# Scores of three sequences moved to the transposes' PSUM banks, with the first stage's steps in another order

## The chip, the cores and the metric

One core of a Trainium2 chip runs the whole kernel. The metric is device time in microseconds (us), the median of three runs; lower is better. One further execution was taken with the hardware profiler. PE is TensorE (matmuls), DVE VectorE, ACT ScalarE, POOL GpSimd, and SP the engine whose queue issues the DMAs here.

## The reference, cut to what matters

An mLSTM cell over 4 batches ("sequences" below) of 8 heads, 768 steps and 40 columns, followed by a two-layer product with an exact GELU between:

```
for t in range(S):                       # per batch and head
    m_new = max(f[t] + m, i[t]);  f_ = exp(f[t] + m - m_new);  i_ = exp(i[t] - m_new)
    C = f_ * C + i_ * outer(v[t], k[t]);  n = f_ * n + i_ * k[t]
    y[t] = sigmoid(o[t]) * (C @ q[t]) / max(abs(n @ q[t]), 1)
x = y.transpose(0, 2, 1, 3).reshape(3072, 320)
out = gelu(x @ w_in) @ w_out             # w_in 320 x 2048, w_out 2048 x 320
```

## The kernel before, in words

The 768 steps are cut into 6 chunks of 128. Within a chunk the recurrence becomes matrix products per sequence: keys and queries are transposed on PE, scores are products of keys and queries (L542), weighted by exponentials W of the gates; the weighted scores meet the values; the state C of the earlier chunks is read and updated; then the output is gated and transposed into x. While one chunk goes through the cell, the chunk before it goes through the two layers: "up" (x by w_in, then Gelu) and "down" (by w_out).

The order of instructions is written out by hand. `play` (L1184) reads a string of words; a word is a letter for a step and a number for the sequence (or the piece) it works on. Each engine executes its own instructions in the order in which the steps issue them, and a wait holds everything behind it on its engine. DMAs stand in SP's queue in the same way. The string FRONT (L27) covers the first chunk's cell, the second chunk's cell, the first chunk's up and down, and the preparation of both weight matrices. DOWN (L34) orders the later chunks, one after another. The change touches FRONT alone and one line of `scores`.

Letters that matter here; lower case is the first chunk, upper case the second:

- m/M masks a W tile on POOL (L440). It comes from DRAM, by `load_M` (L177), in the second chunk and after; word B issues such a load ahead of time. w/W are the exponentials on ACT (L443).
- t/T: four transposes of k and four of q on PE into two banks of the pool `ps_tr`, each copied out on ACT (L514 to L525). `ps_tr` has two banks in all. In the second chunk, T also issues the product of v by a gate on DVE (L529).
- s/S: scores, eight products on PE into two banks, then a product with W on DVE (L532 to L545).
- c/C: products for state and read on PE (L580, L585), then on ACT, or in the second chunk on DVE (L589 to L600).
- v/V: weighted scores by values on PE (L660) into a bank of `ps_h`, and in the second chunk a sum on DVE (L668). y/Y: the gated output, five operations and a copy on DVE (L678 to L696). x/X: its transposes on PE (L707) and a copy on ACT; in the second chunk the bank is in `ps_tr`, and R (L725) on DVE is the last that reads it. g/G: the tanh of the output gate on ACT (L474).
- P fetches a piece of a weight matrix. K and J, each time for the next piece, turn its 64-bit numbers into float32: K on ACT (L373, L374), J on DVE (L385, L386); J also fetches a later piece. Pieces 0 to 9 are w_in, 10 to 25 are w_out. i splits a piece of w_in into a high and a low part (ACT L768, DVE L769), j joins them (DVE L788), h and Z prepare the next up.
- A and U: up-products of the first chunk's first and second half of tokens (L872, L878) into banks "a" or "b" of `ps_mm`, then Gelu on ACT (L882). f2, f3: the rest of that up-product, 24 and 12 products into all four banks of `ps_mm` (L811, L817), then Gelu on ACT (L823). u splits x for them.
- F: one of the 16 rows of the first chunk's down-product (L1111); from F0 on it holds all four banks of `ps_mm`.
- L and O load q, k and v, o_gate. e writes the third chunk's k and q to DRAM and reads them back as blocks. I n puts n idle matmuls into the next bank that a step opens (`unread`, L397); k n puts n matmuls on PE (`warm`, L222).
- E, N, D, Q, d, q compute and transpose the gates; E and N store M to DRAM.

The eight PSUM banks are two of `ps_tr`, two of `ps_h`, and two each of tags "a" and "b" of `ps_mm`. Before the change, the scores of the second chunk's sequences 0 and 2 use "a", those of 1 and 3 `ps_tr` (L540).

Of the kernel before, what the change touches and what calls it, by code (L numbers as in the profile page):

```python
# [24 lines left out]


FRONT = """  # L27
    O0 P0 I4 L0 E P1 I4 P2 w0 L1 t0 O1 L2 k5 K L3 N g0 k2 s0 J w1 D O3 w2 t1 K c0 v0 y0 Q O2 I1 I1 s1 d w3 q
    P3 t2 v1 g1 c1 L4 K J y1 x0 s2 g2 x1 O4 t3 J v2 c2 y2 s3 B4 g3 K x2 B5 T0 v3 J H K y3 K A L5 c3 x3 M1 O7
    O6 K M0 O5 J J u0 u1 G0 L6 W0 S0 i5 W1 A K C0 T1 J J M2 i6 V0 G2 u2 U i7 L7 S1 K G1 K U j5 J j6 j7 i8 W2  # L30
    C1 J K B8 T2 i9 f2 M3 V1 T3 j8 K S2 J h5 Y0 Y1 j9 W3 J C2 K h6 S3 C3 f3 J K Z r X0 J K J K J K V2 V3 h7 K
    F K F Y2 J F K J K J e J G3 R0 h8 J F Z F F X1 F K K F X2 F R1 F J K F J J Y3 K X3 R2 F F F J B9 p R3 F K
    J h9 B10 F"""
DOWN = """  # L34
    M0 F Z F L3 W0 M1 Z W1 S0 C0 F F h0 Q2 F K2 G1 D3 B3 Z V0 G2 M2 W2 M3 W3 V1 K3 Q3 F G0 S2 Z Y0 G3 C2 h2 F
    F Y1 X0 V2 V3 F N F j R0 Y2 Y3 X1 F F X2 R1 F R2 X3 R3 F"""
# [3 lines left out]
def kernel(  # L40
# [18 lines left out]
    B, H, S, D = q.shape  # L59
# [26 lines left out]
    ps_tr = ctx.enter_context(tc.tile_pool(name="ps_tr", bufs=2, space=bass.MemoryType.PSUM))  # L86
    ps_h = ctx.enter_context(tc.tile_pool(name="ps_h", bufs=2, space=bass.MemoryType.PSUM))
    ps_mm = ctx.enter_context(tc.tile_pool(name="ps_mm", bufs=2, space=bass.MemoryType.PSUM))
# [121 lines left out]
    a = gates.tile([BH, NCH, L], F32, name="a")  # L210
# [82 lines left out]
    def decays_last(g0, g1):  # L293
        g = slice(g0, g1)
        pd = ps_tr.tile([P, g1 - g0, BH], F32, name="pd", tag="tr")
        nc.tensor.matmul(pd.rearrange("p c n -> p (c n)"), last, gT[:, g].rearrange("p c n -> p (c n)"),
                         start=True, stop=True)
        by_half = pd.rearrange("p c (n two) -> p c n two", two=2)
        for hip in range(2):
            nc.vector.tensor_copy(out=dec[halves[hip], g], in_=by_half[halves[hip], :, :, hip])  # L300
# [65 lines left out]
    def conv_one(i):  # L366

        if i < len(pieces):
            n = bits[i].shape[1]
            lo, hi = bits[i][:, :, 0], bits[i][:, :, 1]  # L370
            s = sig[i] = raw.tile([P, WP], F32, name="sig", tag="sig")[:, 0:n]
            p = pow2[i] = raw.tile([P, WP], U32, name="pow", tag="pow")[:, 0:n]
            nc.scalar.activation(out=s, in_=hi.bitcast(F32), func=AF.Copy, scale=2.0 ** -112)  # L373
            nc.scalar.activation(out=p, in_=lo, func=AF.Relu, scale=0.9 * 2.0 ** -29, bias=low_bits)  # L374
# [4 lines left out]
    def conv_two(i):  # L379

        if i < len(pieces):
            bits.pop(i)
            to = sig[i] if 4 < i < 10 else pieces[i][1]
            dst, s, p = to.bitcast(U32), (sig[i] if 4 < i < 10 else sig.pop(i)).bitcast(U32), pow2.pop(i)
            nc.vector.scalar_tensor_tensor(out=p, in0=s, scalar=3, in1=p, op0=OP.logical_shift_left, op1=OP.bitwise_or)  # L385
            nc.vector.scalar_tensor_tensor(out=dst, in0=s, scalar=0x80000000, in1=p, op0=OP.bitwise_and, op1=OP.bitwise_or)  # L386
            if i != HELD:
                fetch(i + NB - (i > HELD))
# [8 lines left out]
    def unread(bank):  # L397
        for _ in range(idle[0]):
            nc.tensor.matmul(bank, ident, ident, start=True, stop=True, skip_group_check=True)
        idle[0] = 0  # L400
# [25 lines left out]
    class Cell:  # L426
# [105 lines left out]
        def scores(self, b):  # L532
            n = self.c * B + b
            kT, qT = self.kT.pop(b), self.qT[b]

            pool, tag = (ps_tr, "tr") if self.c > 0 and b % 2 else (ps_mm, "a")
            ps = [pool.tile([P, NP, L], F32, name="ps", tag=tag) for hip in range(2)]
            unread(ps[0][:, 0, :])
            for p in range(NP):
                for hip in range(2):  # L540
                    r = halves[hip]
                    nc.tensor.matmul(ps[hip][:, p, :], kT[r, p, :], qT[r, p, :], start=True, stop=True)  # L542
            for hip in range(2):
                w = W[n].rearrange("p (m two) t -> p m two t", two=2)[:, :, hip, :]
                nc.vector.tensor_tensor(out=w, in0=ps[hip], in1=w, op=OP.mult)  # L545
# [340 lines left out]
    def first_up_steps(h):  # L886

        def step(k):
            ups.append((len(ups) + len(tags_next) % 2, (2 * k, 2 * k + 2, HT * h, HT * h + HT)))
            if len(ups) == 2:  # L890
                first_up()

        return [lambda k=k: step(k) for k in range(HF // 2)]
# [209 lines left out]
    def first_down_steps(g):  # L1103
        po = []

        def row(f):

            if f == 0:
                po.extend(ps_mm.tile([P, DM], F32, name="po", tag="ab"[b // 2]) for b in range(B))
            for b in range(B):  # L1110
                nc.tensor.matmul(po[b], g.t[:, f, b * L:(b + 1) * L], w_out[:, f, :], start=(f == 0),  # L1111
                                 stop=(f == NF - 1))
                if f == NF - 1:
                    if b % 2 == 0:
                        o_sb = outp.tile([P, 2, DM], F32, name="o_sb", tag="o_sb")
                    nc.scalar.copy(out=o_sb[:, b % 2, :], in_=po[b])
                    send(0, b, o_sb[:, b % 2, :])

        return [lambda f=f: row(f) for f in range(NF)]
# [71 lines left out]
    def in_turn(steps):  # L1191
        todo = list(steps)
        return lambda: todo.pop(0)() if todo else None
# [9 lines left out]
    def first_blocks():  # L1203

        copy_chunk(2, range(1))
        for r in (32, 96):
# [7 lines left out]
                 d=lambda: decays_last(0, 1), q=lambda: decays_last(1, NCH - 1), r=halves_out, p=halves_back,  # L1214
                 A=in_turn(first_up_steps(0)), U=in_turn(first_up_steps(1)), e=first_blocks, F=in_turn(first_down_steps(first_g)),
                 K=in_turn(lambda i=i: conv_one(i) for i in n_pieces), H=products_begin,
                 J=in_turn(lambda i=i: conv_two(i) for i in n_pieces), Z=split_weight,
# [47 lines left out]
```

## Time and profile before

| | us |
|---|---|
| median of 3 runs | 460.49 (459.5 to 461.03) |
| profiled execution, its own time | 460.17 |
| its span in the trace | 458.1 |
| PE busy, DVE busy, ACT busy, POOL busy | 446.1, 317.9, 237.7, 77.0 |
| last row F of the front ends on PE | 124.17 |

In a line of the timeline stand the start in us from the span's start, the duration in us, the engine, the line of the kernel, the operation, output and input tiles, shapes and the number of instructions merged; in brackets the idle time of the engine before it, and what ended that. A matmul in float32 counts as two. A line of the stages has, behind the stretch and its length, the busy time and the instructions of PE, PE's weight loads, DVE, ACT and POOL, then the granted clock of PE (1.00 is full), the busy share of the 16 DMA engines and the GB/s that they moved.

### The profile page before, as it was taken

The numbers are of one execution on the slowest core, as the hardware profiler recorded it, in microseconds if no ns is written. First come the engines' busy times: TensorE is split into PE (matmuls) and PEld (weight loads), VectorE is DVE, ScalarE is ACT, GpSimd is POOL, SyncE is SP. The second block draws the span as 40 slices with busy tenths as digits, with TensorE's granted clock in tenths as the row PEclk, the third lists the DMA queues.
The fourth block names the chain that finished last, engine by engine and source line by source line (L and its number), as shares of the span: only waits on it lengthen the run. The fifth ranks groups of instructions, "written<-read, shape, count | busy, mean of one in ns | idle before, by whom it ended". The sixth has DMA issues, their size and how long they took to land.

```text
span 458.1 us, 13016 instructions
## 1 busy us (share of the span) xinstructions
PE 446.1 (97%) x5376; PEld 394.3 (86%) x5376; DVE 317.9 (69%) x672; ACT 237.7 (52%) x541; POOL 77.0 (17%) x117
## 2 busy tenths in 40 slices
PE   8999899999999999999999999999999999999996
PEld 7778687777788988988899988899988898988996
DVE  8797796795469679656488646577646577599940
ACT  4889988972511791203693203594113594257701
POOL 3001130000100433100533100543101512000000
PEclk9999999999999999999999999999999999999999
DMA  7999992479665744139945229942029840200001
GB/s 170 191 222 221 212 242 68 114 188 208 175 160 115 117 61 114 38 56 202 141 88 99 66 44 209 144 80 33 21 51 212 133 87 6 86 30 1 0 2 57
DMA packets 174875, 51.11 MB, mean 112 GB/s; under 512 B 154752, under 2 KB 168352, under 8 KB 174816
## 3 DMA queue, kind: packets, MB, share of 16 engines
q1 hardware_dynamic: 174496, 49.95, 51.6%
q8 instruction: 42, 0.69, 0.6%
q10 hardware_dynamic: 320, 0.33, 0.2%
q14 instruction: 17, 0.14, 0.1%
HBM read 45.47 MB, written 10.03 MB: 121 GB/s over the span
## 4 chain that ended last, share of the span: by engine, by line
PE 86%; ACT 5%; DVE 3%; SPq 3%; DMA 2%; issue 1%; DVEq 0%
PE po L1132 27%; PE pu L1016 23%; PE po L1111 8%; PE pu L1027 6%; PE po L986 6%; PE ph L660 3%; PE ps L558 3%; SPq L152 2%; PE px L707 2%; PE pf L613 2%; ACT W L466 1%; PE pu L811 1%; PE ps L542 1%; PE pf L624 1%; PE cold L225 1%
## 5 line engine op out<-in xcount | busy, mean ns | idle before, releaser
L1132 PE MATMUL po<-w_out,g 128*128 128x160 f32 x512 | 74.4, 302 | 0.0
L1031 ACT ACTIVATE g<-pu 128x512 f32<-128x512 f32 x64 | 32.2, 620 | 81.2 <-PE pu L1027 81.2
L1132 PEld LDWEIGHTS po<-w_out,g 128*128 128x128 f32 x512 | 70.1, 190 | 1.9 <-ACT g L1031 1.3
L466 ACT ACTIVATE W<-W,aT 128x128 f32<-128x128 f32 x128 | 38.7, 388 | 1.2 <-POOL W L440 1.1
L1016 PE MATMUL pu<-x_hi,w_in_hi 128*128 128x512 f32 x160 | 39.0, 387 | 0.0
L440 POOL TENSOR_SCALAR_AFFINE_SELECT W<-W 128x1024 f32<-128x1024 f32 (+2 forms) x20 | 25.2, 1260 | 76.3 <-DMA W<-M_d 75.5
L1132 PE MATMUL po<-w_sums,sums 128*128 128x160 f32 x256 | 36.9, 302 | 0.0
L1132 PEld LDWEIGHTS po<-w_sums,sums 128*128 128x128 f32 x256 | 35.0, 190 | 0.4
L1111 PE MATMUL po<-w_out,g 128*128 128x320 f32 x128 | 35.2, 433 | 0.0
L1016 PEld LDWEIGHTS pu<-x_hi,w_in_hi 128*128 128x128 f32 x160 | 29.5, 189 | 5.7 <-ACT g L1031 1.3
L1111 PEld LDWEIGHTS po<-w_out,g 128*128 128x128 f32 x128 | 24.0, 190 | 9.6
L1016 PE MATMUL pu<-x_all,w_mid 128*128 128x512 f32 x80 | 30.3, 379 | 0.0
L1016 PE MATMUL pu<-x_all,w_in_mid 128*128 128x512 f32 x80 | 30.3, 379 | 0.0
L564 DVE TENSOR_TENSOR W<-ps,W 128x256 f32<-128x256 f32 (+1 forms) x48 | 18.1, 416 | 17.4 <-issue 5.7
L529 POOL TENSOR_TENSOR vw<-vb,ewT 128x328 f32<-128x328 f32 x12 | 8.8, 744 | 122.6 <-DMA vb<-in_v_dram 79.5
L859 DVE TENSOR_TENSOR sums<-g 128x512 f32<-128x512 f32 x16 | 12.8, 800 | 23.2 <-ACT g L1031 23.2
L373 ACT ACTIVATE sig<-bits 128x320 f32<-128x320 f32 (+1 forms) x26 | 15.3, 588 | 12.5 <-DMA bits<-in_moe_w_out_dram 9.1
L385 DVE SCALAR_TENSOR_TENSOR pow<-sig,pow 128x320 uint32<-128x320 uint32 (+1 forms) x26 | 15.5, 596 | 8.0 <-ACT pow L374 8.0
L696 ACT COPY y_rest<-ob 128x128 f32<-128x128 f32 x16 | 4.7, 294 | 30.4 <-DVE ob L689 22.2
L1016 PE MATMUL pu<-x_lo,w_in_lo 128*128 128x512 f32 x80 | 18.9, 379 | 0.0
L1016 PE MATMUL pu<-x_lo,w_in 128*128 128x512 f32 x80 | 18.9, 379 | 0.0
L1132 PE MATMUL po<-t,g 128*128 128x160 f32 x128 | 18.7, 299 | 0.0
(222 smaller groups left out, 968.0 us busy)
## 6 DMA issues: line engine op xcount, KB each, us to landing
W<-M_d SPq DMA_DIRECT2D x16, 512.0 KB, 5.7
bits<-in_moe_w_in_dram SPq DMA_DIRECT2D x20, 256.0 KB, 4.1
bits<-in_moe_w_out_dram SPq DMA_DIRECT2D x16, 320.0 KB, 3.9
blocks<-kq_d SPq DMA_DIRECT2D x32, 128.0 KB, 3.5
ob<-in_o_gate_dram SPq DMA_DIRECT2D x24, 160.0 KB, 4.4
out_dram<-o_sb SPq DMA_DIRECT2D x36, 80.0 KB, 2.0
kq_d<-in_k_dram SPq DMA_DIRECT2D x32, 80.0 KB, 2.5
kq_d<-in_q_dram SPq DMA_DIRECT2D x32, 80.0 KB, 2.6
```

What stands on the lines that cost most here:

```text
L373: nc.scalar.activation(out=s, in_=hi.bitcast(F32), func=AF.Copy, scale=2.0 ** -112)
L385: nc.vector.scalar_tensor_tensor(out=p, in0=s, scalar=3, in1=p, op0=OP.logical_shift_left, op1=OP.bitwise_or)
L440: nc.gpsimd.affine_select(out=x, in_=x, compare_op=OP.is_ge, fill=1.0e30, base=base, pattern=[[0, H], [1, x.shape[2]]], channel_multiplier=-1)
L466: nc.scalar.activation(out=W[n][:, h, :], in_=src, func=AF.Exp, scale=-1.0, bias=aT[:, self.c, r:r + 1])
L558: nc.tensor.matmul(ps[i][hip][halves[x ^ i], p, t], kT[i][r, p, halves[x]], qT[i][r, p, t], start=True, stop=True)
L564: nc.vector.tensor_tensor(out=w[r, :, t], in0=ps[i][hip][r, :, t], in1=w[r, :, t], op=OP.mult)
L986: nc.tensor.matmul(in_pairs(po[t]), x[:, t * L:(t + 1) * L], in_turns(w), start=(f, k) == first, stop=(f, k) == last, skip_group_check=True)
L1016: nc.tensor.matmul(in_pairs(pus[i][e]), w[k][:, e, i * P:(i + 1) * P], in_turns(x[:, k, :]), start=(n == 0 and k == 0), stop=False, skip_g ...
L1027: nc.tensor.matmul(in_pairs(pu[e]), w[r, i // 2, i % 2 * P:(i % 2 + 1) * P], in_turns(x[r, NX, :]), start=False, stop=(n == 2), skip_group ...
L1031: nc.scalar.activation(out=g.t[:, HF * e + i, :], in_=pu[e], func=AF.Gelu, scale=4097.0)
L1111: nc.tensor.matmul(po[b], g.t[:, f, b * L:(b + 1) * L], w_out[:, f, :], start=(f == 0), stop=(f == NF - 1))
L1132: nc.tensor.matmul(bank[k][:, t, :], lhs(j, t), rhs(j), start=(first and t == 0 and j == 0), stop=(t == 1 and j == HF - 1), skip_group_che ...
```

## The change

The scores of sequence b of the second chunk go to the pool `ps_tr` for every b above 0, where it was every odd b. So the code places S2 differently, and S0, S1 and S3 as before. And FRONT is a new string of the same steps: only the fillers differ (I4, I4, I1, I1, k5, k2 before; I4, k1, k7 after; a word I overrides an earlier one that no step has used, so 5 + 7 matmuls before and 4 + 8 after).

```
 FRONT = """
-    O0 P0 I4 L0 E P1 I4 P2 w0 L1 t0 O1 L2 k5 K L3 N g0 k2 s0 J w1 D O3 w2 t1 K c0 v0 y0 Q O2 I1 I1 s1 d w3 q
-    P3 t2 v1 g1 c1 L4 K J y1 x0 s2 g2 x1 O4 t3 J v2 c2 y2 s3 B4 g3 K x2 B5 T0 v3 J H K y3 K A L5 c3 x3 M1 O7
-    O6 K M0 O5 J J u0 u1 G0 L6 W0 S0 i5 W1 A K C0 T1 J J M2 i6 V0 G2 u2 U i7 L7 S1 K G1 K U j5 J j6 j7 i8 W2
-    C1 J K B8 T2 i9 f2 M3 V1 T3 j8 K S2 J h5 Y0 Y1 j9 W3 J C2 K h6 S3 C3 f3 J K Z r X0 J K J K J K V2 V3 h7 K
-    F K F Y2 J F K J K J e J G3 R0 h8 J F Z F F X1 F K K F X2 F R1 F J K F J J Y3 K X3 R2 F F F J B9 p R3 F K
-    J h9 B10 F"""
+    O0 L0 k1 P0 E L1 L2 t0 P1 k7 K w0 g0 N s0 w1 O1 O3 D t1 P2 w2 c0 v0 J y0 Q s1 L3 O2 K d w3 q t2 L4 P3 v1
+    g1 c1 J y1 s2 K x0 t3 x1 v2 g2 O4 J B4 g3 c2 y2 s3 B5 K x2 K L5 J T0 K v3 A y3 M1 x3 c3 G0 M0 H O7 O6 O5 J
+    J i5 u0 L6 u1 K W0 J W1 I4 A K S0 T1 C0 J j5 i6 V0 i7 u2 G2 K U M2 L7 S1 J G1 K U i8 j6 W2 J j7 i9 C1 T2 K
+    M3 f2 S2 V1 Y0 T3 J Y1 C2 j8 W3 j9 e K K K J S3 J C3 f3 K X0 B8 J K R0 B9 h5 J h6 h7 K J V2 K Y2 J J Z Z K
+    K V3 X1 J K r F J h8 h9 F F K F F F F F J K X2 G3 F F J K J F J K Y3 K B10 R1 X3 F p R2 J R3 F F J F F"""
...
-            pool, tag = (ps_tr, "tr") if self.c > 0 and b % 2 else (ps_mm, "a")
+            pool, tag = (ps_tr, "tr") if self.c > 0 and b > 0 else (ps_mm, "a")
```

The changed kernel is one line shorter ahead of every function, so its line numbers are one less (L1131 for L1132).

## The prediction

> **What bounds the kernel now.** I read the page's busy line first, then a table of stages cut where the front's matrix work changes its kind, then, in the timeline, the places where PE waits.
>
> ```profile
> PE 446.1 (97%) x5376; PEld 394.3 (86%) x5376; DVE 317.9 (69%) x672; ACT 237.7 (52%) x541; POOL 77.0 (17%) x117
> ```
> ```profile
> core 0: us, PE busy (x) PEld busy (x) DVE busy (x) ACT busy (x) POOL busy (x), PEclk, DMA share, GB/s
> 0.00:51.58 51.58, 46.89 (x668) 39.64 (x669) 40.89 (x102) 40.92 (x103) 6.58 (x25) 1.00 0.94 197
> 51.58:88.47 36.89, 35.22 (x484) 28.90 (x476) 30.14 (x63) 33.81 (x67) 4.28 (x4) 1.00 0.59 153
> 88.47:124.17 35.70, 35.70 (x145) 25.42 (x139) 22.83 (x53) 17.88 (x40) 2.61 (x3) 1.00 0.79 187
> ```
>
> PE bounds the whole: it is busy for 446.1 us of a span of 458.1, and the change takes no product away. So a gain can only come from PE's idle time in the front, and the reader should see how little that is: 51.58 - 46.89 = 4.69 us up to 51.58, 36.89 - 35.22 = 1.67 up to 88.47, nothing from there to the front's end at 124.17. In the first stage DMA is the scarce thing (share 0.94, then 0.59). Behind the front the code is the same, and I leave its stages as they are.
>
> The cut at 51.58 is a gate. Three engines' rows (POOL, ACT, PE) show it:
>
> ```profile
> 44.32 2.97 POOL L440 TENSOR_SCALAR_AFFINE_SELECT W<-W 128x1024 f32<-128x1024 f32 x2 [39.96 <-DMA W<-M_d]
> 61.70 1.09 POOL L440 TENSOR_SCALAR_AFFINE_SELECT W<-W 128x1024 f32<-128x1024 f32 x1 [14.42 <-DMA W<-M_d]
> ```
> ```profile
> 47.32 2.45 ACT L466 ACTIVATE W<-W,aT 128x128 f32<-128x128 f32 x8 [1.09 <-POOL W L440]
> 49.67 0.62 ACT L768 ACTIVATE hi_first<-sig 128x512 fp32r<-128x512 f32 x1
> 50.19 0.68 ACT L466 ACTIVATE W<-W,aT 128x128 f32<-128x128 f32 x2
> ```
> ```profile
> 50.91 0.74 PE L660 MATMUL ph<-vb,W 128*32 128x41 f32 x56 [0.32 <-DVE W L545]
> 51.58 3.72 PE L872 MATMUL pu<-first_x,w_in 128*128 128x256 f32 x16
> 55.23 1.13 PE L878 MATMUL pu<-first_x,w_rest 64*128 64x256 f32 x8
> 57.23 1.16 PE L542 MATMUL ps<-qT,kT 64*128 64x128 f32 x16 [0.86 <-ACT qT L523]
> ```
>
> POOL had sat idle for 39.96 us until the W transfers landed; masks M1 and M0, the exponentials W0, DVE's product of S0 and the matmuls V0 follow one another, and PE goes on with U at 51.58. In both orders the same bytes stand ahead of these two transfers on SP's queue, where they are the 39th and 40th transfer. **The gate is DMA's, and nothing that PE does earlier passes it.**
>
> **The change, part by part.** *1. Ahead of V0.* The new order loads q and k of sequences 1 and 2 ahead of the second piece of w_in, and PE gets through v0 to v3 sooner. By an estimate from the durations of before, PE ends the second up-product A 1 to 2.5 us sooner; then come four filling matmuls (moved there: 12 fillers in both orders), S0, T1 and C0, and at V0 it waits for the gate. What was won is idled away: 0. Bounds: DMA has dips of its own ahead of the transfers, of which this is one,
>
> ```profile
> 37.00:38.00 1.00, 1.00 (x6) 0.87 (x6) 0.93 (x5) 0.85 (x3) 0.00 (x0) 1.00 0.63 102
> ```
>
> 0.37 us; without two or three such, W lands 1 us sooner. Against that, the second store of M_d stands six entries earlier on SP, where it must wait for DVE's scans, and the loads behind it (v and o_gate first) wait too: 0.7 us at most, if the queue runs dry. So -1.0 to +0.7.
>
> *2. From V0's end to F0, the first row of the down-product.* PE's steps are the same; only waits count. Before, they are the 1.67 us of gaps, and a stretch hidden in "busy" at S2. PE's rows, and one of ACT:
>
> ```profile
> 71.92 0.82 PE L660 MATMUL ph<-vb,W 128*32 128x41 f32 x64
> 72.67 1.09 PE L520 MATMUL pt<-ident,qk 128*128 128x128 f32 x8
> 74.57 1.65 PE L542 MATMUL ps<-qT,kT 64*128 64x128 f32 x16 [0.80 <-ACT g L823]
> 76.14 0.67 PE L580 MATMUL pf<-vw,kb 128*64 128x41 f32 x16
> ...
> 79.61 1.99 PE L811 MATMUL pu<-first_x_hi,hi_first 128*128 128x512 f32 x8
> ...
> 86.48 0.44 PE L707 MATMUL px<-ident,ob 128*128 128x128 f32 x2
> ```
> ```profile
> 71.45 0.63 ACT L523 COPY qT<-pt 128x512 f32<-128x512 f32 x1
> ```
>
> S1 above took 1.16 us undisturbed; S2 takes 1.65 after 0.80 of waiting, because its two "a" banks hold sums of f2 until their Gelus have run. So 0.49 more is wait: 1.67 + 0.49 = 2.16 us.
>
> In the new order:
> - S1: the split i5 (50.19 - 49.67 = 0.52 on ACT) no longer stands between W0 and W1, so T1's copies come 0.52 sooner. PE waits 0.86 - 0.52 = 0.34, and f2 ends at 71.92 - 0.52 = 71.4.
> - S2 stands right behind f2, in the transposes' banks. It needs T2's copies, which ended at 71.45 + 0.63 = 72.08 behind K10 and now stand ahead of it: about 70.5. No wait; 0.80 + 0.49 go.
> - Late next: T3 takes those two banks back, so now it waits for DVE's product of S2. S2 ends at 72.5, the product's halves at 73.1 and 73.8; PE, with V1 (72.67 - 71.92 = 0.75), is there at 73.25: 0.1. Behind T3 on PE stand C2, S3, C3 and f3, so this wait holds everything.
> - From there DVE's queue is the second bound. Its prices, from two stretches, and one row disturbed by POOL:
>
> ```profile
> 81.39 0.68 DVE L788 TENSOR_TENSOR mid_two<-hi_first,w_in 128x512 fp32r<-128x512 f32 x1
> 81.99 0.48 DVE L385 SCALAR_TENSOR_TENSOR pow<-sig,pow 128x320 uint32<-128x320 uint32 x1
> 82.51 0.49 DVE L386 SCALAR_TENSOR_TENSOR w_out<-sig,pow 128x320 uint32<-128x320 uint32 x1
> 82.92 0.49 DVE L589 TENSOR_TENSOR far<-pf,gT 128x328 f32<-128x328 f32 x1
> 83.33 0.65 DVE L598 TENSOR_TENSOR state<-state,dec 64x164 f32<-64x164 f32 x2
> 84.02 0.32 DVE L600 TENSOR_TENSOR state<-state,pf 128x164 f32<-128x164 f32 x1
> 84.26 0.68 DVE L545 TENSOR_TENSOR W<-ps,W 128x512 f32<-128x512 f32 x1
> ```
> ```profile
> 78.23 0.48 DVE L678 SCALAR_TENSOR_TENSOR ob<-ob,far 128x320 f32<-128x320 f32 x1
> ...
> 79.80 0.23 DVE L696 COPY y_rest<-ob 128x128 f32<-128x128 f32 x1
> ```
> ```profile
> 61.91 1.43 DVE L788 TENSOR_TENSOR mid_two<-hi_first,w_in 128x512 fp32r<-128x512 f32 x1
> ```
>
>   A join is 0.68, a J step 82.92 - 81.99 = 0.93, DVE's part of a C step 84.26 - 82.92 = 1.34, a product of scores two halves, 1.3, a 128x328 operation 0.49, a Y step 78.23 to 80.03, 1.80. Behind 72.5 stand S2's product, V1's sum, Y0, the v product of sequence 3, J10, Y1 without its copy, C2, and the joins j8 and j9: 1.3 + 0.49 + 1.80 + 0.49 + 0.93 + 1.57 + 1.34 + 1.36 = 9.3, so 81.8. On PE, T3 (some 1.0) and C2, S3, C3 (79.61 - 76.14 = 3.47) bring f3 to 77.8; its third group of eight (8 in some 1.8 us) wants both joins at 81.4: 0.4 of wait.
> - J11, S3's product, J12 and C3 follow on DVE: 0.93 + 1.3 + 0.93 + 1.34 = 4.5, so 86.3. V3 needs the bank that C3 read. PE: f3 takes 86.48 - 79.61 = 6.87 and ends at 85.1, X0 and V2 take 1.1, so 86.2: 0.1. POOL's v product for the third chunk falls near there, and while POOL ran at 61.70 a join took 1.43 rather than 0.68. One such hit adds 0.75, none 0; I take 0.3, together 0.4. (The Trainium skill, GPSIMD Engine Reference, section 1, Specifications: its SBUF interfaces are shared with VectorE, with contention where DVE has two SBUF inputs. By that rule the hit is certain, and the gain below would be 0.45 us smaller.)
>
> New waits: 0.34 + 0.1 + 0.4 + 0.4 = 1.2 us. Gain: 2.16 - 1.2 = **0.9 us**, from 0.5 (POOL's hit) to 1.6 (DVE quick, only S1's wait and a little left). X1 now stands before F0 rather than among the rows F: neither gain nor loss.
>
> *3. The down-product.* It is dense now. Rows of PE, DVE and ACT:
>
> ```profile
> 113.24 10.93 PE L1111 MATMUL po<-w_out,g 128*128 128x320 f32 x40
> ```
> ```profile
> 111.64 0.55 DVE L730 SCALAR_TENSOR_TENSOR x_lo<-px,x_hi 128x384 fp32r<-128x384 f32 x1
> ```
> ```profile
> 114.71 0.49 ACT L373 ACTIVATE sig<-bits 128x320 f32<-128x320 f32 x1 [5.82 <-DMA bits<-in_moe_w_out_dram]
> ```
>
> Five rows F in 10.93: 2.2 each. The pieces of w_out come through SP's queue. Two W loads (B8, B9) move ahead of most of them; the store and reload of the third chunk's blocks (e) moves out of this stretch into the quiet time before f3, where SP stalls for it and PE doesn't. Closest to PE stands X3: its bank waits for R1 on DVE, which stands behind Y3, which stands behind J23; on ACT, K23 stands behind X2's copy. From X2 on: copy 0.5, tanh 0.4, K23 1.0, J23 0.9, Y3 1.8, R1 two of 0.55: 5.7 us, beside F8, F9 and F10, 6.5. Hidden by 0.8; if that cover goes, each us is a us. Value: 0.
>
> Sum, against the profiled execution (460.17 us, span 458.1): 460.17 - 0.9 = 459.3. The median of the three runs, 460.49, is 0.3 above it; between the two scales I take **459.4**.
>
> **The rivals.** *B, the gate moves:* W lands 1 us sooner, PE idles less before V0, and the 0.9 stays: 460.2 - 1.9 = 458.3; with 1.6 in part 2, 457.6. For it: PE is early there. Against it: SP's new wait for the scans. *C, the hand-over eats it:* DVE is 0.9 us later than summed, and T3, f3 and V3 each wait: 460.2. For it: DVE is busy for 30.14 of 36.89 us in this stage. *D, slower:* X3 behind R1, Y3 and J23. It decides when piece 23 lands after about 107; I get 105.8 (an estimate: some 1.2 us a piece and 2.4 a W load from 85.4, when X0 frees SP). At 1.7 a piece it is 110 to 111, X3 comes 3 us late, and the kernel ends at 462.3. For it: ACT waited 5.82 us for such a piece at 114.71. Against it: e is gone from this stretch. *E, it doesn't do what it says:* S2 still waits, for T2's copies; they would have to be 1 us later than summed. It ends as C does.
>
> PE's idle time before V0 would grow to some 1.6 us in one piece; the clock is 1.00 in all stages. (The Trainium skill, TensorE: Matmul & The Clock Gate, Part 1, halves the clock after an idle window of about 3.4 us. By that, 1.6 us is too short and nothing changes. No run shows it yet.)
>
> **How the numbers follow.** A measurement of this kernel can tell about 0.3%, 1.4 us, from no change: under 459.1 is faster, over 461.9 slower. My forecast A has 0.42 (its own range 458.5 to 460.1, 0.16 of it under 459.1); B 0.23, nearly all faster (0.22); C with E 0.15, within; D 0.20, slower. Faster 0.16 + 0.22 = 0.38; within 0.26 + 0.01 + 0.15 = 0.42; slower 0.20. Range 457.4 (just under B's end) to 462.3 (D).
>
> **What would show it.** S2's wait for a Gelu gone, T3 or V3 waiting for DVE in its place; V0 ending at 51.6 within 1 us, behind POOL's masks, with PE's idle time before it in one piece; F0 at 87.6 to 88.2 with X1 before it; no wait of PE at X3. I am wrong if V0 ends more than 1 us from 51.6, if f3 waits for more than 1 us, or if a stage behind the front, which I left alone, moves by more than the front does.

## The result, and the profile after

The changed kernel takes **459.27 us** (median of 21 runs, 457.36 to 460.25), the kernel before 460.73 (21 runs, 458.9 to 462.19). The ratio is **0.997, 95% interval 0.9958 to 0.9981**: 0.3% faster, just at the bound that I had set. The number forecast, 459.4, is 0.1 us off. The trace shows that it came out by errors of opposite sign.

The profiled execution of the changed kernel took 459.76 us (span 458.0). Its stages, cut at the same times as those of before, columns as there:

```profile
core 0: us, PE busy (x) PEld busy (x) DVE busy (x) ACT busy (x) POOL busy (x), PEclk, DMA share, GB/s
0.00:51.58 51.58, 47.69 (x647) 40.43 (x651) 40.89 (x104) 40.99 (x104) 5.75 (x25) 0.97 0.95 199
51.58:88.47 36.89, 36.49 (x525) 30.09 (x513) 28.28 (x65) 35.41 (x69) 4.81 (x5) 1.00 0.70 168
88.47:124.17 35.70, 35.70 (x139) 25.60 (x138) 21.79 (x51) 17.87 (x40) 1.78 (x2) 1.00 0.67 180
```

In the second row PE is idle for 0.40 us, where it was idle for 1.67 and waited 0.49 more inside its busy time. In the first row PE looks busier than before (47.69, was 46.89), but its clock is **0.97**, which was 1.00: some of that busy time is slow work.

PE's rows in the timeline, from V0 to the end of the front:

```profile
51.15 0.82 PE L659 MATMUL ph<-vb,W 128*32 128x41 f32 x64
51.90 3.72 PE L871 MATMUL pu<-first_x,w_in 128*128 128x256 f32 x16
...
57.00 1.16 PE L541 MATMUL ps<-qT,kT 64*128 64x128 f32 x16 [0.31 <-ACT qT L522]
...
71.60 1.05 PE L541 MATMUL ps<-qT,kT 64*128 64x128 f32 x16
72.58 0.82 PE L659 MATMUL ph<-vb,W 128*32 128x41 f32 x64
73.49 1.25 PE L519 MATMUL pt<-ident,qk 128*128 128x128 f32 x8
...
78.14 1.99 PE L810 MATMUL pu<-first_x_hi,hi_first 128*128 128x512 f32 x8
...
81.70 1.89 PE L810 MATMUL pu<-x_all,mid_two 128*128 128x512 f32 x8
...
87.38 2.86 PE L1110 MATMUL po<-w_out,g 128*128 128x320 f32 x10
```
```profile
111.40 0.38 PE L706 MATMUL px<-ident,ob 128*128 128x128 f32 x2
...
111.72 10.93 PE L1110 MATMUL po<-w_out,g 128*128 128x320 f32 x40
122.25 1.92 PE L1015 MATMUL pu<-x_hi,w_in_hi 128*128 128x512 f32 x7
```

S1 waits 0.31, S2 follows f2 with no gap, T3 begins 0.09 after V1's end and takes 1.25 rather than 1.09, and everything from there to 122.25, where the second chunk's up begins, is dense. In the kernel before the same point was at 123.77:

```profile
123.77 1.48 PE L1016 MATMUL pu<-x_hi,w_in_hi 128*128 128x512 f32 x5
```

So the front is 1.52 us shorter. V0 ends at 51.90, **0.32 later** than the 51.58 of before; from there to 122.25 pass 70.35 us instead of 72.19, **1.84 less**.

Behind the front the code is the same, but this execution took 335.75 us for it (458.0 - 122.25), the one of before 334.33. PE's waits say where the difference could lie; the changed kernel's first, then those of before, the first two rows of each:

```profile
engine line waited for: us in total, times, longest us
PE ph L659 <- issue: 2.6, 3, 1.5
PE pt L519 <- DVE ewT L251: 1.5, 1, 1.5
```
```profile
PE ph L660 <- issue: 1.4, 2, 0.7
PE ph L660 <- DVE W L545: 1.2, 2, 0.8
```

"issue" are waits with no releaser in the profile, all behind the front: 2.6 us here, 1.4 before. The stretch behind the front took 334.3 to 334.9 in four traces of kernels with the old string FRONT (two with one step moved), and 334.6 to 336.3 in ten with the new one or an edit of it. It moves by up to 2 us between traces, though its code is the same in all, so a single profiled execution can't settle 1.5 us in this kernel: the front has to be compared with the front. Whether the new string also lengthens it by some half a microsecond on average is open.

**The new thing is ahead of V0.** In the second row of the changed kernel's waits stand 1.5 us in one piece: t1 stands right behind D and needs the two banks that D has just filled. The stretch in the changed kernel, microsecond by microsecond, columns as in the stages:

```profile
14.00:15.00 1.00, 0.38 (x4) 0.26 (x3) 1.00 (x2) 0.92 (x2) 0.00 (x0) 1.00 1.04 326
15.00:16.00 1.00, 0.12 (x1) 0.12 (x2) 1.00 (x5) 1.00 (x5) 0.00 (x0) 1.00 1.08 282
16.00:17.00 1.00, 1.00 (x9) 0.94 (x10) 1.00 (x2) 1.00 (x5) 0.00 (x0) 0.82 1.20 204
17.00:18.00 1.00, 1.00 (x8) 0.72 (x7) 0.71 (x2) 1.00 (x3) 0.00 (x0) 0.50 1.14 185
...
19.00:20.00 1.00, 1.00 (x22) 1.00 (x22) 0.00 (x0) 1.00 (x5) 0.00 (x0) 0.50 1.01 261
20.00:21.00 1.00, 1.00 (x33) 0.95 (x30) 0.00 (x0) 0.96 (x4) 0.00 (x0) 0.98 0.96 227
```

PE is idle from 14.38 to 15.88, and from about 16.6 to 20.0 its clock is 0.50. In the kernel before, w2 stood between D and t1 and cut this time into waits of 0.49 and 0.43, and the clock stayed at 1.00. 15 of the 21 runs of the changed kernel have a mean clock of 0.995 or 0.996 and a median of **459.47**; the other 6 (0.999 or 1.0) have **457.98**.

**And V0's gate moved.** POOL, ACT, DVE and PE ahead of V0 in the changed kernel:

```profile
42.71 2.13 POOL L439 TENSOR_SCALAR_AFFINE_SELECT W<-W 128x1024 f32<-128x1024 f32 x2 [38.35 <-DMA W<-M_d]
```
```profile
41.07 1.08 ACT L881 ACTIVATE g<-pu 128x512 f32<-128x512 f32 x2 [0.89 <-PE pu L877]
...
46.31 1.28 ACT L465 ACT_TABLE_LOAD   x1
47.60 4.79 ACT L465 ACTIVATE W<-W,aT 128x128 f32<-128x128 f32 x16
```
```profile
49.85 1.29 DVE L544 TENSOR_TENSOR W<-ps,W 128x512 f32<-128x512 f32 x2 [0.72 <-ACT W L465]
```
```profile
46.76 1.16 PE L398 MATMUL ps<-ident 128*128 128x128 f32 x8
```

The W transfers landed 1.6 us sooner (42.71, was 44.32), and the masks end at 44.84. W0 begins only at 47.60, with no idle time on ACT just before it: its own queue, which begins with the Gelu of A, is what is late, and that Gelu (41.07) had waited 0.89 us for A, which is PE's. The DVE product ends at 51.14 and V0 begins at 51.15; the four fillers at 46.76 fit almost exactly into the time that PE would have waited. So V0 hangs on PE in this execution, whose clock was low. At a full clock another link comes last, as e1 and e6 show below.

### The profile page after: what moved, and what is told of

Same layout as the page of the kernel before. It is cut to its first block, busy times and chain, and to the rows that moved or that the text cites. A ratio compares the mean times of both kernels' runs of the same rounds, so it can differ in the third digit from the quotient of the medians.

```text
span 458.0 us, 13012 instructions
## 1 busy us (share of the span) xinstructions
PE 446.6 (98%) x5376; PEld 395.1 (86%) x5376; DVE 314.1 (69%) x672; ACT 237.9 (52%) x541; POOL 74.9 (16%) x117
## 4 chain that ended last, share of the span: by engine, by line
PE 88%; ACT 3%; DVE 2%; issue 1%; DMA 1%; SPq 1%; DVEq 0%
PE po L1131 27%; PE pu L1015 23%; PE po L1110 8%; PE pu L1026 6%; PE po L985 6%; PE ph L659 4%; PE ps L557 3%; PE pu L810 2%; PE pf L612 2%; PE px L706 2%; PE pu L871 2%; PE pt L519 1%; ACT W L465 1%; PE pf L623 1%; DMA ob<-in_o_gate_dram 1%
## 5 line engine op out<-in xcount | busy, mean ns | idle before, releaser
L1131 PE MATMUL po<-w_out,g 128*128 128x160 f32 x512 | 74.4, 302 | 0.0
L1131 PEld LDWEIGHTS po<-w_out,g 128*128 128x128 f32 x512 | 70.1, 190 | 1.9 <-ACT g L1030 1.3
L1131 PE MATMUL po<-w_sums,sums 128*128 128x160 f32 x256 | 36.9, 302 | 0.0
L439 POOL TENSOR_SCALAR_AFFINE_SELECT W<-W 128x1024 f32<-128x1024 f32 (+2 forms) x20 | 24.2, 1215 | 77.4 <-DMA W<-M_d 59.4
L1131 PEld LDWEIGHTS po<-w_sums,sums 128*128 128x128 f32 x256 | 35.0, 190 | 0.4
L1131 PE MATMUL po<-t,g 128*128 128x160 f32 x128 | 18.7, 299 | 0.0
```

The costliest lines, as they stand in the source:

```text
L439: nc.gpsimd.affine_select(out=x, in_=x, compare_op=OP.is_ge, fill=1.0e30, base=base, pattern=[[0, H], [1, x.shape[2]]], channel_multiplier=-1)
L1131: nc.tensor.matmul(bank[k][:, t, :], lhs(j, t), rhs(j), start=(first and t == 0 and j == 0), stop=(t == 1 and j == HF - 1), skip_group_che ...
```

## The experiments

Theory: (1) behind V0, the bank and the order gain 1.8 us together and neither does alone; (2) ahead of V0, the idle stretch at t1 halves the clock in most runs, and that costs 1.5 us; (3) V0 hangs on ACT's queue, which follows PE. Rivals: the order alone, or the bank alone, makes the gain; the W transfers hold V0 whatever PE does, as I had forecast.

**e1, the old bank in the new order.**

```
-pool, tag = (ps_tr, "tr") if self.c > 0 and b > 0 else (ps_mm, "a")
+pool, tag = (ps_tr, "tr") if self.c > 0 and b % 2 else (ps_mm, "a")
```

> The changed kernel with its new order, but S2 back in the two "a" banks. My theory: the bank is needed for this order. S2 stands right behind f2, whose Gelus read the "a" banks; in the changed kernel f2 ends at 71.60 and the first two Gelus end at about 73.2, so the second half of S2 starts there and S2 ends at about 74.3 rather than 72.6; T3's wait of 0.16 goes. The front ends 1.5 us later than in the changed kernel: 460.8, ratio to before 1.000, and the trace shows PE waiting for the Gelu of f2 at S2. Rival, the order alone gives the gain and the bank is worth nothing: 459.3, ratio 0.997.

Measured: 460.66, ratio 1.0002 (0.9985 to 1.0019). PE's row for S2:

```profile
71.73 1.64 PE L541 MATMUL ps<-qT,kT 64*128 64x128 f32 x16 [1.25 <-ACT g L822]
```

The Gelu's wait is back, 1.25 us and 0.6 in the length of S2. At equal clocks it is 459.51 against 457.98 (clock 0.999 and more) and 460.81 against 459.47: 1.5 and 1.3 us, as the theory said. (The kernel before had 460.73 beside the changed kernel, 460.26 beside e1 to e4, 459.65 beside e5 to e8 and 460.39 beside e9 to e12, so times of different groups compare to about 1 us; the ratios don't have this error.)

"Neither alone" is a little too strong. The profiled execution of e1 has a clock of 1.00. Its V0 ends at 50.93 and the second chunk's up begins at 122.65, which is 71.72 us, where it was 72.19 before and 70.35 in the changed kernel: behind V0 the order alone gains 0.47 and the bank in it 1.37 more. In the whole time nothing is left of that, since 6 of the 12 runs have a low clock; the other 6 have 459.51, where the kernel before had 460.26.

Up to V0 the code of e1 is the changed kernel's, so this execution also shows the gate with the clock undisturbed. V0 ends 0.65 sooner than before. It waited 1.16 us for DVE, where the first pair of the split of x took 1.58 and 1.57 while POOL masked (42.82 to 45.93), and the second pair 0.68 each behind that.

**e2, the new bank in the old order.**

```
-pool, tag = (ps_tr, "tr") if self.c > 0 and b % 2 else (ps_mm, "a")
+pool, tag = (ps_tr, "tr") if self.c > 0 and b > 0 else (ps_mm, "a")
```

> The kernel before with its old order, but S2 in the transposes' banks. My theory: in the old order S2 stands behind T3, so it needs the banks that T3 has just filled; T3's two copies on ACT stand behind f2's Gelus and end at 76.3 + 0.65 = 76.96 in before, so S2 starts near 77.0 rather than 75.0 and the kernel is 1.9 us slower than before: 462.6, ratio 1.004. Rival, the bank is worth S2's 0.80 + 0.49 us of waiting in either order: 459.4, ratio 0.997.

Measured: 464.58, ratio 1.0081 (1.0054 to 1.0109).

```profile
75.08 1.65 PE L542 MATMUL ps<-qT,kT 64*128 64x128 f32 x16 [1.84 <-ACT kT L523]
```

The wait is where I put it, for T3's copies, and the bank without its order costs time. The sizes are off: from V0's end to F0 the trace (at a clock of 1.0) lost 1.15 us and not 1.9, since S2 starts when the first copy is done. Four of the six runs have a clock of 0.992 to 0.996 and 464.4 to 465.6; the two at 1.0 have 461.34 and 462.33. An idle stretch of 1.84 us again comes with runs at a low clock, a cost that I had left out; the profiled execution is one of the two at 1.0, so no trace shows where the clock fell in the others.

**e3, e7 and e6, a bridge over the idle stretch:** 11, 3 and 6 filling matmuls between D and t1.

```
-w1 O1 O3 D t1 P2 w2
+w1 O1 O3 D k11 t1 P2 w2        (k3, k6)
```

> The changed kernel with 11 filling matmuls between D and t1, where PE sat idle for 1.50 us and the granted clock then fell to 0.50 from 16.8 to 20.0 us. My theory: the idle stretch brings the clock down, and the slow 3.3 us cost 1.5 us, which go on through PE, the Gelu of A, ACT's queue and W0 to V0. With the bridge the clock stays at 1.00, V0 ends near 50.4 rather than 51.9, and the time is 457.8, ratio 0.9935. Rival, V0 is held by the W transfers and the masks whatever PE does earlier: the clock is back at 1.00, but V0 still ends at 51.9 and the time stays at 459.3, ratio 0.997. Second rival, the clock falls for another reason: granted clock 0.50 at 17 to 20 us as now, 459.3.

> The changed kernel with 3 filling matmuls ahead of t1: 0.70 us of work, so 0.8 us of the idle stretch stay. It asks how long a stretch halves the clock. If idle time of 0.8 us is too short (the kernel before has stretches of 0.48, 0.49 and 0.43 at a clock of 1.00): clock 0.999 or 1.0 in nearly all runs and 457.9, ratio 0.9935. If 0.8 us is enough: clock 0.995 to 0.996 in most runs, 459.4, ratio 0.997.

> The changed kernel with 6 filling matmuls ahead of t1, where the earlier bridge had 11. The 11 took 2.56 us, 0.233 each, so 6 take 1.40, just the idle stretch of 1.50. My theory: clock at 1.00 in nearly all runs, and t1 starts 1.06 us sooner than behind 11; all of PE's work up to V0 follows, since the Gelu of A and ACT's queue behind it follow PE: 457.3 to 457.9, ratio 0.993. Rival, V0 is held by something that PE doesn't set, so the bridge's length is hidden: 458.3, ratio 0.9946 as with 11.

Measured: with 11, 458.31, ratio 0.9946 (0.9925 to 0.9967); with 3, 458.31, 0.996 (0.9943 to 0.9978); with 6, **457.78, 0.9948 (0.9926 to 0.997)**. The clock was below 0.998 in 2 of 12, 1 of 10 and 0 of 10 runs. PE's rows with 3 and with 6:

```profile
14.04 0.93 PE L224 MATMUL cold<-w_out 128*128 128x128 f32 x6
15.60 0.66 PE L519 MATMUL pt<-ident,kb 128*128 128x128 f32 x4 [0.64 <-DVE ewT L251]
```
```profile
14.09 1.61 PE L224 MATMUL cold<-w_out 128*128 128x128 f32 x12
15.64 0.66 PE L519 MATMUL pt<-ident,kb 128*128 128x128 f32 x4
...
17.02 0.39 PE L460 MATMUL pm<-M_parts,row 96*128 96x128 bf16 x4
```

The group with L460 takes 0.39 here and 0.63 in the changed kernel. V0 ends at 50.40 with 6 (at 50.72 with 11, 50.34 with 3), 1.5 us sooner than in the profiled execution of the changed kernel, so the rival that V0 is held by the W transfers whatever PE does falls for these kernels: with 6 the masks end at 44.71 and W0 begins at 46.14. But ACT's queue doesn't follow PE any more. With 6 it begins with a wait for a piece of w_in:

```profile
33.03 0.68 ACT L372 ACTIVATE sig<-bits 128x512 f32<-128x512 f32 x1 [1.37 <-DMA bits<-in_moe_w_in_dram]
...
46.14 4.79 ACT L465 ACTIVATE W<-W,aT 128x128 f32<-128x128 f32 x16
```

From there to W0 it runs without a gap for 13.11 us, and so it does in e1 (33.18 to 46.29). So theory (3) holds for the low clock; at a full clock, in these two, the first link is a transfer again, of a piece of w_in and not of W. With 11 and 3 fillers the Gelu of A still waits for PE, 0.58 and 0.19 us, less than the 0.89 in the changed kernel.

Idle time of 0.64 us was followed by a low mean clock in 1 of 10 runs only. The kernel with 6 has the lowest median and no run at a low clock, but by the ratios it can't be told from those with 11 and 3, nor from the changed kernel: all these intervals overlap. At a full clock the changed kernel runs in 457.98 and this one in 457.78: what the bridge gives is the clock, and no more.

**e4, no fillers ahead of S0.**

```
-u1 K W0 J W1 I4 A K S0
+u1 K W0 J W1 A K S0
```

> The changed kernel without the four filling matmuls ahead of S0 (1.09 us on PE). My theory: V0 is held by DVE's product of S0, which waits for the exponentials W0 on ACT, so PE idles 1.1 us before V0 and V0 still ends at 51.9: 459.3, ratio 0.997. Rival, PE itself is the bound ahead of V0: V0 ends at 50.8, 458.2, ratio 0.9945. Second rival, the new idle stretch of 1.1 us brings the granted clock to 0.50 for some 3 us behind V0: 460.7, ratio 1.000.

Measured: 460.17, ratio 0.999 (0.9971 to 1.0009).

```profile
50.31 0.28 PE L659 MATMUL ph<-vb,W 128*32 128x41 f32 x8 [0.67 <-DVE W L544]
50.90 0.74 PE L659 MATMUL ph<-vb,W 128*32 128x41 f32 x56 [0.31 <-DVE W L544]
51.58 3.72 PE L871 MATMUL pu<-first_x,w_in 128*128 128x256 f32 x16
```

PE now waits 0.98 us for DVE's product, and from the end of A to the end of V0 pass 5.04 us (46.54 to 51.58), where it was 5.07 (46.83 to 51.90): the fillers cost nothing ahead of V0, as the theory said, and PE by itself isn't the bound there. The new wait started no slow stretch behind V0 in this trace (clock 1.00 from 50 to 60). The median is 0.9 above the changed kernel's, and 0.7 above it at a low clock (460.21 against 459.47); in the trace the front is 0.25 shorter and the unchanged part behind it the longest of all, 336.3, with "issue" waits of 3.3 us. The intervals of the two ratios overlap, so this 0.7 may be noise; I can't explain it.

**e5, w2 ahead of t1 again.**

```
-w1 O1 O3 D t1 P2 w2 c0
+w1 O1 O3 D P2 w2 t1 c0
```

> The changed kernel with P2 and w2 ahead of t1, as the order was before the change. My theory: the four groups of matmuls of w2 fill the stretch in which t1 waits for D's banks, so the one idle stretch of 1.5 us becomes two of at most 0.5 (0.49 and 0.43 in before), the granted clock no longer falls to half after it, and the matmuls of w2 are done earlier by about 0.4 us. Time 457.5 (the runs of the changed kernel at a clock of 0.999 or 1.0 have a median of 457.97, less 0.4), ratio 0.993. Rival, the clock falls for something other than this idle stretch: most runs at a clock of 0.995 and 459.1 or more, ratio 0.997.

Measured: 458.57, ratio 0.9964 (0.9941 to 0.9986).

```profile
15.36 0.38 PE L460 MATMUL pm<-M_parts,row 96*128 96x128 bf16 x4 [1.70 <-ACT W L465]
```

A miss: in the new order w1's exponentials end later on ACT, and w2 waits for their bank in one piece of 1.70 us. The clock is low in 6 of 12 runs, with 459.19 against 457.74. So it speaks for the idle stretch as the cause all the same: another waiting step, as long a stretch, and the clock is low again. In its profiled execution (clock 1.00) the W transfers landed at 44.05, W0 waited 0.88 for the masks, and V0 ended at 51.36: in the new order too the transfers can still come last.

**e12, the kernel before with t1 ahead of w2:** the suspected step of the change alone.

```
-w1 D O3 w2 t1 K c0
+w1 D O3 t1 w2 K c0
```

> The kernel before with one edit: t1 ahead of w2, as the change has it. My theory: PE then waits at t1 in one piece, about 2.0 us (D's last matmul ends at 15.4, D's copies on DVE at 17.1), where it had two waits of 0.49 and 0.43, and the granted clock falls to 0.50 for 3.4 us in most runs (mean 0.995 to 0.996). Ahead of V0 PE had 1.2 us to spare in the kernel before, so of the 0.9 us of later w2 and the 1.5 us of slow clock only about 1.2 show: 461.7, ratio 1.003, and at a full clock no change. Rival: this swap is not what brings the clock down (the fewer filling matmuls ahead of it are): clock 0.999 or 1.0 in most runs, 460.3, ratio 1.000.

Measured: 461.62, ratio 1.0044 (1.0019 to 1.0069).

```profile
17.58 0.66 PE L520 MATMUL pt<-ident,kb 128*128 128x128 f32 x4 [1.61 <-DVE ewT L252]
```

One stretch of 1.61 us instead of 0.49 and 0.43, and the clock is low in 6 of 12 runs (462.69 against 460.72); in the runs of the kernel before beside these experiments it was low in 4 of 77. The swap alone brings it, and the time is what I expected (461.7).

**e8 and e11, ACT's queue ahead of V0 shortened.** Both leave out the fillers ahead of S0. e8 stands on e5, e11 on e6.

```
-u1 K W0 J W1 I4 A K S0 T1 C0 J j5
+u1 W0 W1 A S0 T1 K J C0 K J j5             (e8)
+u1 W0 K W1 A S0 J T1 K C0 J j5             (e11)
```

> The run with w2 ahead of t1, and in front of V0 the step K (1.42 us on ACT) moved from ahead of W0 to behind T1's copies, its J behind S0's product on DVE, and the four filling matmuls ahead of S0 left out. My theory: at V0 and S1 the last to come is ACT's queue (W0, W1, the Gelu of A, T1's copies), no longer the W transfers: the second mask ended at 44.84 and W0 began at 47.60. So W0 begins up to 1.4 us sooner, V0 ends 1.1 us sooner, S1 follows, and the time is 1.1 us under the run with w2 ahead of t1 alone: 456.4, ratio 0.991. Rival, the transfers and masks still hold V0: no change against that run, 457.5, ratio 0.993. Second rival, the moved J makes i6 and the second group of f2 late: slower by up to 1.5 us, 459, with PE waiting in f2.

> The run with 6 filling matmuls ahead of t1, and in front of V0 one K (1.42 us on ACT) moved from ahead of W0 to behind it, the next K behind T1's copies, the J of the first behind S0's product, and no filling matmuls ahead of S0. My theory: with the clock at 1.00 in both, ACT's queue and PE are the last to come at V0 and S1; W0 begins 1.0 to 1.4 us sooner if the masks allow it (they end 0.1 to 0.5 us before that), V0 ends 0.8 us sooner, T1's copies come 1.4 us sooner and S1 waits no more: 456.9, ratio 0.993. Rival, the W transfers and the masks hold W0: V0 no earlier, 457.8, ratio 0.9948. Second rival, DVE, whose second J comes 1.2 us later, delays S1's product, and T2 waits for that: 458.5 or more.

Measured: e8 464.1, ratio 1.0085 (1.0058 to 1.0113), clock low in 6 of 6 runs; e11 458.65, ratio 0.997 (0.9953 to 0.9987), low in none of 12. ACT and PE in e8:

```profile
48.42 4.78 ACT L465 ACTIVATE W<-W,aT 128x128 f32<-128x128 f32 x16 [1.52 <-POOL W L439]
```
```profile
67.75 1.11 PE L519 MATMUL pt<-ident,kb 128*128 128x128 f32 x4 [3.49 <-DVE W L544]
```

In e8 the W transfers landed at 45.26, and the masks were the gate again; then DVE stood still for a late load of v (2.75 us) and for the moved K (2.61), S1's product behind them was late, and T2 waited 3.49. In e11 V0 ended at 49.05, 1.35 before e6. But at S3 its lead is gone:

```profile
74.18 1.05 PE L541 MATMUL ps<-qT,kT 64*128 64x128 f32 x14 [0.64 <-ACT qT L522]
```

T3's copies stand behind f2's Gelu, and that began on ACT at 71.10, against 70.90 in e6: ACT (35.57 us busy of 36.89 in this stage) wasn't a bit earlier, and F0 is at 85.73 against 85.92. ACT's queue is the next bound behind V0. Both were misses: I had expected 456.4 and 456.9.

**e9, i5 alone, and e10, the joins pushed back.** One execution each.

```
-W0 S0 i5 W1 A K C0             (e9, on the kernel before)
+W0 S0 W1 i5 A K C0
-C2 j8 W3 j9 e K K K J S3 J C3  (e10, on the changed kernel)
+C2 K J j8 W3 j9 e K K J S3 C3
```

> The kernel before, with one edit: i5 behind W1 instead of between W0 and W1. It measures the first half of the gain behind V0 by itself, in the trace. My theory: the split on ACT (0.52 us) no longer stands ahead of W1 and T1's copies, so PE's wait at S1 falls from 0.86 to 0.34 us, and S2's wait for the Gelu of f2 (0.80, and 1.65 rather than 1.16 for S2 itself) stays. Rival: the wait at S1 hangs on something else on ACT (the Gelu of A or a K that waits for its piece) and stays at 0.8 or more.

> The changed kernel with one K J pair moved ahead of the joins j8 and j9, so that 0.93 us more stand on DVE ahead of them. It measures how much cover f3 has, where I forecast 0.4 us of waiting and saw none. In the changed kernel the joins end at 81.48 and the third group of f3 starts at 81.70. My theory: the cover is just these 0.22 us, so f3 now waits 0.93 - 0.22 = 0.7 us at its third group. Rival: the joins are not what the third group needs at its start, and f3 stays dense (6.87 us).

e9 doesn't measure what it should: behind W1, i5 still stands ahead of the Gelu of A and of T1's copies, and S1 waited 0.90. Its price must be read from ACT's rows: from W0's begin to the end of T1's copies pass 9.86 us in the kernel before (47.32 to 57.18), 9.89 in e9 and 9.34 in the changed kernel (47.60 to 56.94), where i5 stands ahead of W0. That is 0.52 less, the length of the split. In e10, f3's third group:

```profile
81.49 2.38 PE L810 MATMUL pu<-x_all,mid_two 128*128 128x512 f32 x8
```

It took 0.49 more and began 0.15 late: f3 lasts 7.51 (77.78 to 85.29) instead of 6.87. 0.64 us of wait for 0.93 of DVE work: the cover was 0.3, where the theory had 0.22.

**What they show of the clock.** The runs of all these kernels, by the longest idle stretch of PE between 10 and 25 us in the profile:

| longest idle stretch, us | kernels | runs with a clock below 0.998 |
|---|---|---|
| 1.48 to 1.70 | changed, e1, e4, e5, e12 | 43 of 69 |
| 0.64 | e7 | 1 of 10 |
| 0.5 | e3, e6, e11 | 2 of 34 |
| 0.5 | before, beside the experiments | 4 of 77 |

(e2 and e8 have long waits elsewhere too and are left out, and e10 is a single run.) The clock here is the mean of a run; it tells that the clock fell, not where. Within one kernel the runs at a low clock take 1.3 (e1), 1.45 (e5), 1.49 (changed) and 1.97 us (e12) longer.

## Why the prediction was right or wrong

- **What bounds: right.** PE is busy for nearly the whole span in all kernels, and the gain came out of its idle time in the front.
- **Part 1, the value 0 ahead of V0: wrong, and this is the step that failed.** "The gate is DMA's, and nothing that PE does earlier passes it" held for the kernel before and not for the profiled execution of the changed one. The W transfers landed 1.6 us sooner, and then ACT's queue was last, in which the Gelu of A had waited 0.89 for PE. At a full clock half of the sentence comes back: in e1 and e6 ACT's queue ahead of W0 begins with a wait for a piece of w_in, so its first link is DMA's, though not the W transfers. These landed at 41.7 to 45.3 in the traces with the new order, and the later of these (e5, e8) did hold W0. V0 ends 0.65 us sooner in e1, whose code is the same up to there, and 1.2 sooner in e6 (50.93 and 50.40, against 51.58): rival B's gate moved, by about the 1 us that I gave it. PE didn't idle for 1.6 us before V0; its fillers filled 1.09 of that and cost nothing there (e4).
- **What hid this was a step that I had left at nothing:** t1 moved ahead of w2. I had counted its instructions and not the banks that it takes over from D. The price is 1.5 us in 15 of 21 runs, by the clock. In the profiled run V0 came 0.32 later and not 0.65 to 1.2 sooner. My sentence on the clock looked at the wrong place, V0, and at a bound that is too lenient: I held idle time of 1.6 us for too short, and 1.50 us was enough.
- **Part 2: the mechanism right, its size off by two terms.** Gained were 1.8 us and not 0.9. S1's wait was 0.31 (0.34 forecast), S2's 0.80 + 0.49 went, T3's new wait was 0.09 ahead of it and 0.16 inside it (0.1). The two waits of 0.4 at f3 and V3 did not come. At f3 the joins came 0.2 to 0.3 us ahead of the third group (e10), while my sum had them 0.4 behind: the rows of DVE that I had summed to 9.3 take 8.74 in the changed kernel (72.74 to 81.48), since each begins a little before the one ahead has ended, and PE reached the third group at 81.70, not 81.4. Rows of DVE, PE and POOL in the changed kernel at V3:

```profile
85.54 0.33 DVE L599 TENSOR_TENSOR state<-state,pf 128x164 f32<-128x164 f32 x1
```
```profile
86.26 0.81 PE L659 MATMUL ph<-v,W 128*32 128x41 f32 x64
```
```profile
86.92 0.74 POOL L528 TENSOR_TENSOR vw<-vb,ewT 128x328 f32<-128x328 f32 x1 [20.43 <-DVE w_out L385]
```

  C3's bank was read 0.4 us before PE needed it, and POOL's product, the hit that I had feared, came behind it, with DVE idle. That the two disturb each other is so: in e8 an operation on DVE took 1.58 us beside POOL's masks and 0.68 just behind them. In e10 the feared hit came, but too late for V3: an operation of J at 86.02 took 1.03, not 0.49, beside POOL's product. (The Trainium skill, GPSIMD Engine Reference, section 1, Specifications, says the same of the shared interfaces; with it I called the hit certain, and in the changed kernel POOL came too late for it.)
- **Part 3: right.** The bank of X3 was free at 110.8 (R1's last row on DVE: 110.25 and 0.55 long) and X3 began at 111.40: a cover of 0.6, forecast 0.8. The rivals C, D and E did not happen.
- **The sum** came out by luck, because the terms missed cancel for the most part: 0.9 too little gained in part 2, and 0.3 lost instead of 0 in part 1, the net of an earlier gate and a low clock; a gain of 1.5 in the front, and 1.46 between the medians (460.73 - 459.27). So the gain was 0.56 above the 0.9 forecast; 0.43 of that doesn't show in the number, since I started from 460.3 (459.4 + 0.9), between the profiled execution and the median of three runs, and the median of 21 is 460.73. In the profiled executions alone (460.17 and 459.76), the part behind the front takes 1.4 back. The 6 runs in which the clock didn't fall have 457.98, the place of rival B.

## What to carry to other kernels

A bank and the order of steps around it are one change: here, behind V0, the order alone gained 0.47 us, the bank alone cost 1.15 up to F0, and both together gave 1.84 (as whole kernels 1.0002, 1.0081 and 0.997). When a step is moved, write down which banks it takes over and who reads them last; a wait that had been cut into short pieces may come together in one. And look at the granted clock of each stretch and each run before trusting a sum of durations: a gap on PE is paid twice when the clock falls behind it, and here fillers bought that back, already when they took 0.93 us of a gap of 1.5.

## What the runs showed of the hardware

With an idle stretch of PE of 1.5 to 1.7 us, the mean clock was below 0.998 in 43 of 69 runs; with stretches of 0.64 us and less in 7 of 121. Where the clock falls is seen in the profiled executions with a low mean: to 0.50, 0.2 to 0.8 us after the end of that stretch, for 3.4 us (16.6 to 20.0 in the changed kernel, 15.9 to 19.3 in e4; e10 and e8 alike). e8 has a second such stretch of 3.4 us (67.6 to 71.0), as its wait of 3.49 at T2 ends. By these numbers one takes 3.4 x 0.5 / 458 = 0.004 off a run's mean, which is the 0.995 to 0.996 of most runs at a low clock. The same stretch of 1.48 us in the profiled run of e1 was not followed by it:

```profile
13.00:14.00 1.00, 0.57 (x5) 0.26 (x3) 1.00 (x3) 0.83 (x2) 0.00 (x0) 1.00 0.95 246
14.00:15.00 1.00, 0.00 (x0) 0.00 (x0) 1.00 (x4) 1.00 (x5) 0.00 (x0) 1.00 0.90 296
...
16.00:17.00 1.00, 1.00 (x14) 0.61 (x11) 0.87 (x2) 1.00 (x4) 0.00 (x0) 1.00 1.05 181
```

So one profile at a clock of 1.00 doesn't show that a gap is safe. The Trainium skill (TensorE: Matmul & The Clock Gate, Part 1, "What's actually happening") has activity judged in windows of about 3.4 us that run free of the kernel. The length of the slow stretch agrees, and a free-running window would explain why the same gap is punished in some runs only; that is argued and not shown. That it takes an idle window of about 3.4 us disagrees: half of that was enough.
